# A 2-D transform pair rebuilt on a half spectrum with half-sample shift, in an adaLN block with its backward pass

## The chip, the cores and the metric

The program runs on one core of one Trainium2 chip. The metric is the device time of one execution in microseconds (us), as the median of several runs. Besides those runs there is one profiled execution; its rows are what this document reads. PE is TensorE (matmul), PEld its weight loads, DVE is VectorE, ACT ScalarE, POOL GpSimd, SP the engine that issues the DMAs. L12 is line 12 of the kernel.

## The reference

One block of a conditioned network and its whole gradient, S = 2048 positions, D = 512 features, F = 1792 hidden units, bf16:

```python
mod = silu(c) @ w_mod                # six rows of 512: sa, ca, ga, sb, cb, gb
h   = layernorm(x) * (1 + ca) + sa
y   = irfft2(rfft2(h) * (w_r + 1j*w_i))      # 2-D FFT over (2048, 512)
x1  = x + ga * y
h2  = layernorm(x1) * (1 + cb) + sb
out = x1 + gb * (relu(h2 @ w1 + b1)**2 @ w2 + b2)
```

It returns out and the gradients of x, w_r, w_i, w1, b1, w2, b2, c and w_mod for a given grad_out. The backward pass of the filter is the same kind of work as the forward one: a 2-D transform of the gradient of y, a product with the conjugate of the filter, and an inverse transform.

## The kernel before

Rows: position s = 16p + t, so x is 16 tiles ("rows", t) of 128 partitions by 512 features. The 2048-point transform over s is split in 128 x 16, and every step of it is a matmul against a table of cosines and sines.

*Constants.* `trig3_from_index` (L26) makes a cosine, a sine and a negative sine from a table of products of indices: scale, round to the nearest integer and subtract (VectorE), then ScalarE's Sin. `build_constants_pre` (L44) makes TA (128-point table, 5 x 128 columns), `build_constants_cd_lc` (L88) makes Cd (512-point table: cos, sin, -sin for 257 frequencies) and LC (the twiddles and the 16-point step in one, masked to blocks of 8), `build_constants_cf` (L133) makes Cf (inverse 512-point table). Their iotas run on GpSimd.

*Modulation* (L425 to L458): w_mod (3 MB) is loaded, six rows of 512 computed and broadcast over the partitions into `modb`.

*LayerNorm 1* (L479 to L492): per row a tensor_reduce on VectorE and a Square with a running sum on ScalarE, then a handful of ops for 16 rows at once with a square root on ScalarE. `h1_row` (L494) normalises one row on ScalarE, stores it to `n1_dram` and applies 1 + ca and sa with two tensor_tensor ops on VectorE.

*Forward transform.* Stage 1, `spec_stage_a` (L180): 16 rows x 4 feature chunks, each a matmul against 256 columns (cos and -sin of TA), each evicted from PSUM, VectorE and ScalarE in turn, into UT. Stages 2 and 3, `spec_stages_bc` (L196): for each of 16 frequency groups 16 matmuls of 257 columns (the 512-point step, real and imaginary apart), two evictions, 4 matmuls of 257 columns against LC, two evictions, and six VectorE ops of 257 columns for the complex product with the filter (`load_wf`, L255, scales the filter by a row `ef` first). In the backward pass the same function also makes the filter's gradients with six more.

*Inverse transform.* `spec_stage_a2` (L271): 16 groups x 3 frequency chunks, two matmuls of 256 columns each. `spec_stages_b2c2` (L289): for each of 16 rows 12 matmuls of 512 columns into psDr and psDi, an eviction of each (ScalarE, VectorE), two matmuls of 512 columns into psY, and the row's consumer. In the forward pass that is `y_cons` (L517): copy y, store it, x1 = x + ga*y, LayerNorm 2 of the row with a Square, a reduce and seven small ops, scale and shift, four transposes into h2T. In the backward pass it is `gh1_cons` (around L855 to L878): the gradient through LayerNorm 1, six VectorE ops of 512 columns and two column sums on TensorE.

*The rest*: MLP 1 (L560 to L584), MLP 2 with the loss side of the gradient (L588 to L650), the MLP's backward pass (L655 on; it begins with a 2 MB load of the normalised rows into n2b, L658, from which VectorE rebuilds h2b, L662, and with the matmuls psg, L681), the gradient of w1 (L780 to L805, its matmuls psw at L799), then the backward transforms (L812 to L880) and the gradients of w_mod by chunks (`emit_gmod_chunk`, L338). The tables live until MLP 2 has ended, are stored to DRAM after MLP 1 (`cs_dram`, L586) and reloaded before the backward transforms (L813).

*Order.* A planner lists each engine's instructions by its own estimate of when they are ready; an instruction whose data and memory are free may stand far ahead of its place in the text, DMAs above all. At run time every engine works through its list in order. Tiles that lie in the same memory at different times wait for one another; "left" and "right" are two ends of the on-chip memory from which pools are taken. All DMAs go through SP's queue.

## Time and profile before

| | |
|---|---|
| median of 3 runs | 847.06 us (845.75 to 848.27) |
| span of the profiled execution | 846.4 us, 10536 instructions; no time besides it is given for that execution |
| PE busy | 671.8 us (79%), 3600 instructions |
| DVE busy | 541.6 us (64%), 1569 |
| ACT busy | 328.4 us (39%), 695 |
| POOL busy | 5.0 us (1%), 17 |
| DMA | 87.71 MB, mean 104 GB/s |

The stages follow one another with little overlap: tables, modulation and LayerNorm sums (0 to 52 us), forward stage 1 (52 to 80), stages 2 and 3 (80 to 122), inverse first stage (122 to 143.5), inverse row loop (143.5 to 210), MLP 1 and 2 (210 to 332), a gap (332 to 350), MLP backward (350 to 645), then the same transform stages backward (645 to 676, 676 to 718, 718 to 743, 743 to 812) and the last chunks (812 to 846.4). The page's shares are of the whole span, so the stages are read one by one: a view of busy time by stretch gives the limit of each, the chain of waits what ended last, the timeline the pace of single instructions. Matmuls are pipelined; where a mean duration is above the pace, the pace is taken from starts that follow one another.

### The profile page before, as it was taken

The numbers are of one execution on the slowest core, as the hardware profiler recorded it, in microseconds if no ns is written. First come the engines' busy times: TensorE is split into PE (matmuls) and PEld (weight loads), VectorE is DVE, ScalarE is ACT, GpSimd is POOL, SyncE is SP. The second block draws the span as 40 slices with busy tenths as digits, with TensorE's granted clock in tenths as the row PEclk, the third lists the DMA queues.
The fourth block names the chain that finished last, engine by engine and source line by source line (L and its number), as shares of the span: only waits on it lengthen the run. The fifth ranks groups of instructions, "written<-read, shape, count | busy, mean of one in ns | idle before, by whom it ended". The sixth has DMA issues, their size and how long they took to land. (4 is left out here: it accounts for less than half of the span.)

```text
span 846.4 us, 10536 instructions
## 1 busy us (share of the span) xinstructions
PE 671.8 (79%) x3600; PEld 313.8 (37%) x3644; DVE 541.6 (64%) x1569; ACT 328.4 (39%) x695; POOL 5.0 (1%) x17
## 2 busy tenths in 40 slices
PE   3137988996999997599999789948997599699940
PEld 0013763332444433254444323305553277233300
DVE  7986875997444455845454369973123469879881
ACT  5985434786676311133333101124132335332210
POOL 1000000000000000000000000000000000000000
PEclk9555998997999999699999979957999599899955
DMA  6433003443634234422221543220154540200010
GB/s 256 180 130 111 34 1 113 135 136 122 239 148 174 87 94 160 145 69 88 69 88 44 67 145 112 88 74 12 39 192 182 168 189 2 100 13 32 31 50 25
DMA packets 56073, 87.71 MB, mean 104 GB/s; under 512 B 9810, under 2 KB 48596, under 8 KB 53972
## 3 DMA queue, kind: packets, MB, share of 16 engines
q1 hardware_dynamic: 56020, 87.05, 30.2%
q8 instruction: 28, 0.46, 0.2%
q14 instruction: 25, 0.20, 0.1%
HBM read 50.27 MB, written 36.76 MB: 103 GB/s over the span
## 5 line engine op out<-in xcount | busy, mean ns | idle before, releaser
L684 DVE SCALAR_TENSOR_TENSOR ghT<-rT_pf,twof,psg 128x512 bf16<-128x512 bf16 x56 | 40.7, 744 | 51.4 <-PE psg L681 51.2
L681 PE MATMUL psg<-gBT,w2T 128*128 128x512 bf16 x218 | 60.1, 389 | 2.3 <-ACT gwm L362 1.8
L740 PE MATMUL psh<-w1T,ghT 128*128 128x512 bf16 x218 | 55.5, 391 | 1.0 <-issue 0.5
L621 PE MATMUL psO<-w,hactT 128*128 128x512 bf16 x217 | 52.7, 379 | 1.1 <-ACT rT L580 0.8
L577 PE MATMUL psH<-h2T,w 128*128 128x512 bf16 x219 | 51.7, 386 | 2.1 <-ACT rT L580 1.0
L799 PE MATMUL psw<-ghn,h2b 128*128 128x448 bf16 x256 | 51.4, 354 | 0.0
L700 PE MATMUL psw<-gB,hnat 128*128 128x512 bf16 x216 | 50.2, 380 | 1.0 <-DVE hnat L697 0.5
L186 PE MATMUL psA<-TA,h1row 128*128 128x256 bf16 x64 | 18.8, 402 | 36.5 <-DVE h1row L501 33.8
L580 ACT ACTIVATE rT<-psH,b1col 128x512 bf16<-128x512 f32 x56 | 38.4, 687 | 15.8 <-PE psH L577 14.4
L581 DVE TENSOR_TENSOR hactT<-rT 128x512 bf16<-128x512 bf16 x56 | 23.8, 426 | 32.1 <-ACT rT L580 32.1
L702 ACT CAST gw<-psw 128x512 bf16<-128x512 f32 x14 | 8.2, 586 | 73.8 <-PE psw L700 63.2
L304 PE MATMUL psDi<-Cf,U2T 128*128 128x512 bf16 (+1 forms) x94 | 35.5, 378 | 0.1
L303 PE MATMUL psDr<-Cf,U2T 128*128 128x512 bf16 (+1 forms) x92 | 35.0, 381 | 0.5 <-ACT U2T L286 0.4
L740 PEld LDWEIGHTS <-ghT 128*128 128x128 bf16 x224 | 19.9, 99 | 40.4 <-issue 22.6
L743 ACT CAST gh<-psh 128x512 bf16<-128x512 f32 x16 | 9.4, 586 | 65.0 <-PE psh L740 65.0
L695 ACT COPY rnat<-pstr 128x512 bf16<-128x512 bf16 x56 | 29.9, 588 | 12.1 <-PE pstr L694 10.1
L303 PE MATMUL psDr<-Cf_reload,U2T 128*128 128x512 bf16 (+1 forms) x93 | 33.8, 381 | 0.9 <-ACT U2T L286 0.4
L304 PE MATMUL psDi<-Cf_reload,U2T 128*128 128x512 bf16 (+1 forms) x95 | 34.1, 379 | 0.1
L191 ACT CAST UT<-psA 128x256 bf16<-128x256 f32 x64 | 23.0, 371 | 27.7 <-PE psA L186 26.9
L577 PEld LDWEIGHTS <-w 128*128 128x128 bf16 x224 | 22.0, 98 | 31.2 <-issue 8.9
L799 PEld LDWEIGHTS <-h2b 128*128 128x128 bf16 x256 | 24.6, 98 | 20.8 <-issue 0.2
L303 PEld LDWEIGHTS <-U2T 128*128 128x128 bf16 (+1 forms) x192 | 17.9, 95 | 38.3 <-issue 24.5
(289 smaller groups left out, 1442.0 us busy)
## 6 DMA issues: line engine op xcount, KB each, us to landing
rT_dram<-rT SPq DMA_DIRECT2D x14, 512.0 KB, 2.6
rT_pf<-rT_dram SPq DMA_DIRECT2D x14, 512.0 KB, 3.4
w<-in_B_w_dram SPq DMA_DIRECT2D x2, 1792.0 KB, 7.2
wm<-in_w_mod_dram SPq DMA_DIRECT2D x1, 3072.0 KB, 10.2
wmc_pf<-in_w_mod_dram SPq DMA_DIRECT2D x6, 512.0 KB, 14.4
...
```

The costliest lines, as they stand in the source:

```text
L303: nc.tensor.matmul(psDr, lhsT=lhsT, rhs=Cf[:ksz, (0 if ri == 0 else 2), fs, :], start=(n == 0), stop=(n == 5))
L304: nc.tensor.matmul(psDi, lhsT=lhsT, rhs=Cf[:ksz, (1 if ri == 0 else 0), fs, :], start=(n == 0), stop=(n == 5))
L577: nc.tensor.matmul(psH, lhsT=w1[:, dc, fc * P:(fc + 1) * P], rhs=h2T[:, dc, sc * 4 * P:(sc + 1) * 4 * P], start=(dc == 0), stop=(dc == 3))
L580: nc.scalar.activation(rT[:, sc * 4 * P:(sc + 1) * 4 * P], psH, AF.Relu, bias=b1col[:, fc:fc + 1])
L581: nc.vector.tensor_tensor(hactT[fc][:, sc * 4 * P:(sc + 1) * 4 * P], rT[:, sc * 4 * P:(sc + 1) * 4 * P], rT[:, sc * 4 * P:(sc + 1) * 4 * P ...
L621: nc.tensor.matmul(psO, lhsT=hactT[fc][:, t * P:(t + 1) * P], rhs=w2[:, fc, :], start=(fc == 0), stop=(fc == NFC - 1))
L681: nc.tensor.matmul(psg, lhsT=w2T[:, dc, fc * P:(fc + 1) * P], rhs=gBT[:, dc, sc * 4 * P:(sc + 1) * 4 * P], start=(dc == 0), stop=(dc == 3))
L684: nc.vector.scalar_tensor_tensor(out=ghT[fc][:, sc * 4 * P:(sc + 1) * 4 * P], in0=rT[:, sc * 4 * P:(sc + 1) * 4 * P], scalar=K["twof"], in ...
L695: nc.scalar.copy(out=rnat[:, 4 * tg:4 * tg + 4, :], in_=pst.rearrange("p (j f) -> p j f", j=4))
L700: nc.tensor.matmul(psw2, lhsT=hnat[:, t, :], rhs=gB[:, t, :], start=(t == 0), stop=(t == NT - 1))
L740: nc.tensor.matmul(psh, lhsT=ghT[fc][:, t * P:(t + 1) * P], rhs=w1T[:, fc, :], start=(fc == 0), stop=(fc == NFC - 1))
L799: nc.tensor.matmul(psw, lhsT=h2[:, t, dc * P:(dc + 1) * P], rhs=ghn[:, t, cc * 448:(cc + 1) * 448], start=(t == 0), stop=(t == NT - 1))
```

## The change

Both transforms are computed on a half spectrum with a half-sample shift. The 512-point step uses angles 2 pi f (d + 1/2) / 512; cosines of even index and sines are each 256 columns, so the real input gives 512 real columns and not 2 x 257 complex ones, and the first step over s (TA) is one real table of 128 columns (`build_ta`), of which TAT is the transpose for the last step. Frequency groups go in pairs (g, 16 - g); LF and LG hold the twiddles with the combination of a pair, 6 and 3 tables of 16 x 128 and 16 x 256 columns. All tables are made from integer indices (multiply, add, bitwise and) and one Sin with a bias.

- Constants: `build_basic`, `build_ta`, `build_cd`, `build_cf`, `build_lf`, `build_lg` take the place of the three builders. GpSimd makes iotas, masks and small vectors.
- x is loaded first, in four pieces; w_mod after it, in four.
- LayerNorm 1 and 2: `bn_stats` and `bn_aggr` on VectorE, `rstd` (an add and a power -0.5) on GpSimd, one tensor_scalar (subtract, multiply) on VectorE.
- 1 + ca, sa and ga are multiplied into the tables CdF (forward) and CdB (backward); sa enters through one extra matmul of one row. 1 + cb and sb are applied in the eviction of the transposed rows. The modulation is computed after stage 1.
- Stage 1 `spec_f1`, stages 2 and 3 `spec_f23` with `cmul`, inverse `spec_g1` and `spec_g23` take the place of the four `spec_stage...` functions.
- LF, LG, CdB and Cf (7.3 MB) are stored right after they are built and reloaded in the backward pass (before: 3.7 MB). The tables' memory is released before the hidden activations are allocated.
- Backward: g_x1 is loaded in four pieces and used directly as the input of stage 1; before, its rows were loaded a second time and multiplied by ga. n1 is loaded in the pool of the last stage. The spectrum Xs is stored to DRAM by group.

The MLP and its backward pass are not edited, but for the release of the tables. The core of the diff:

```diff
-        for t in range(NT):
-            nc.vector.tensor_reduce(ssum[:, t:t + 1], x_sb[:, t, :], axis=AX.X, op=ALU.add)
-            nc.scalar.activation(n1junk, x_sb[:, t, :], AF.Square, accum_out=ssq[:, t:t + 1])
+        def n1_row(t):
+            nc.vector.bn_stats(st, x_sb[:, t, :])
+            nc.vector.bn_aggr(mv, st)
+            rstd(nc, inv1[:, t:t + 1], mv[:, 1:2], K)
+            nc.vector.tensor_scalar(n1row, x_sb[:, t, :], mv[:, 0:1], inv1[:, t:t + 1], op0=ALU.subtract, op1=ALU.mult)
+            nc.sync.dma_start(n1_dram[:, t, :], n1row)
+            return n1row
+def rstd(nc, dst, var, K):
+    nc.gpsimd.tensor_scalar(dst, var, 1e-5, None, op0=ALU.add)
+    nc.gpsimd.tensor_tensor(dst, dst, K["nhalf"], op=ALU.pow)
...
+def build_lf(tc, K, cpool, g):
...
+    for nm, off in (("c", 1536.0), ("s", 1024.0)):
+        v = g.tile([P, 16, P], I32, name=f"lf_v{nm}")
+        nc.vector.tensor_scalar(v, kr, tf, off, op0=ALU.mult, op1=ALU.add)
+        nc.vector.tensor_single_scalar(v, v, 2047, op=ALU.bitwise_and)
+        w = g.tile([P, 16, 16, 8], BF16, name=f"lf_{nm}")
+        nc.scalar.activation(w.rearrange("p g a b -> p g (a b)"), v, AF.Sin, scale=TWO_PI / 2048, bias=K["npi"])
+        tr.append(w)
...
+    for y, (w, m) in enumerate(((c, 0), (s, 1), (s, 2), (c, 2), (c, 1), (s, 3))):
+        nc.vector.tensor_tensor(L5[:, y], w, mk[:, m, :, None, :].broadcast_to([P, 16, 16, 8]), op=ALU.mult)
...
+def spec_f1(tc, K, row, UT):
...
+            ps = psA_pool.tile([P, 4, P], FP32, name="psA")
+            for c in range(4):
+                nc.tensor.matmul(ps[:, c, :], lhsT=hrow[:, c * P:(c + 1) * P], rhs=K["TA"], start=True, stop=True)
+            if t % 2 == 1:
+                nc.scalar.copy(out=dst, in_=src)
+            else:
+                nc.vector.tensor_copy(out=dst, in_=src)
+def spec_f23(tc, K, UT, Cd, dc, dest, elementwise):
...
+        def f3(gi):
+            ae = AEs[gi % 3]
+            for g in pair_of(gi):
+                ps = psC_pool.tile([P, 2, 512], FP32, name="psC")
+                for o, ys in ((0, (0, 1, 2, 3)), (1, (1, 4, 3, 5))):
+                    for n, y in enumerate(ys):
+                        ri, e = n // 2, n % 2
+                        nc.tensor.matmul(ps[:, o, 0:DF], lhsT=LF[:, y, g, :], rhs=ae[:, ri, 256 * e:256 * e + DF],
+                                         start=(n == 0), stop=(n == 3))
+                nc.scalar.copy(out=dest(g), in_=ps[:, :, 0:DF])
+            elementwise(gi)
+        for gi in range(8):
+            for ri in range(2):
+                for c in range(4):
+                    nc.tensor.matmul(ps[:, ri, :], lhsT=UT[:, c, ri * 8 + gi, :, :], rhs=Cd[:, c, :],
+                                     start=(c == 0), stop=(c == 3 and not extra))
...
+            nc.scalar.copy(out=dst, in_=ps.rearrange("p r (e f) -> p r e f", e=2))
+            if gi > 0:
+                f3(gi - 1)
+        f3(7)
+def cmul(nc, pool, A, B, gi, outr, outi, conj_a, nm):
+    sl = pair_slice(gi)
+    nc.vector.tensor_tensor(p1[:, :, :, 0:DF], A[:, sl, :, 0:DF], B[:, sl, :, 0:DF], op=ALU.mult)
+    nc.vector.tensor_tensor(p2[:, :, :, 0:DF], A[:, sl, :, 0:DF], B[:, sl, ::-1, 0:DF], op=ALU.mult)
+    nc.vector.tensor_tensor(outr[:, sl], p1[:, :, 0, 0:DF], p1[:, :, 1, 0:DF], op=(ALU.add if conj_a else ALU.subtract))
+    nc.vector.tensor_tensor(outi[:, sl], p2[:, :, 0, 0:DF], p2[:, :, 1, 0:DF], op=(ALU.subtract if conj_a else ALU.add))
+def spec_g1(tc, K, Z, CS):
...
+        for gi in range(8):
+            for e in range(2):
+                for ch in range(2):
+                    for g in pair_of(gi):
+                        for ri in range(2):
+                            nc.tensor.matmul(ps[:, ch, :], lhsT=Z[:, g, ri, f0:f0 + P],
+                                             rhs=LG[:, e + ri, g].rearrange("p r t b -> p (r t b)"),
+                                             start=(n == 0), stop=(n == 3))
+def spec_g23(tc, K, CS, consumer):
...
+        def g3(t, Tsb):
+            psY = psY_pool.tile([P, D], FP32, name="psY")
+            nc.tensor.matmul(psY, lhsT=K["TAT"], rhs=Tsb, start=True, stop=True)
+            consumer(t, psY)
+        for t in range(NT):
+            for c in range(4):
+                nc.tensor.matmul(ps, lhsT=CS[:, t, c].rearrange("p r a b -> p (r a b)"), rhs=K["Cf"][:, c, :],
+                                 start=(c == 0), stop=(c == 3))
+            nc.scalar.copy(out=Tsb, in_=ps)
+            if prev is not None:
+                g3(*prev)
...
+            rstd(nc, inv2[:, t:t + 1], mv[:, 1:2], K)
+            nc.vector.tensor_scalar(n2rows[:, t % 4, :], x1row, mv[:, 0:1], inv2[:, t:t + 1], op0=ALU.subtract, op1=ALU.mult)
+            if t % 4 == 3:
...
+                    if dc % 2 == 0:
+                        nc.vector.tensor_scalar(dst, src, cbcol[:, dc:dc + 1], sbcol[:, dc:dc + 1], op0=ALU.mult, op1=ALU.add)
+                    else:
+                        nc.scalar.activation(dst, src, AF.Identity, scale=cbcol[:, dc:dc + 1], bias=sbcol[:, dc:dc + 1])
...
-                def u_row(t):
-                    nc.sync.dma_start(gr, gx1_dram[:, t, :])
-                    nc.vector.tensor_tensor(ur, gr, modb[:, 2, :], op=ALU.mult)
+            spec_f1(tc, K, lambda t: g_x1[:, t, :], UT)
```

## Rows read from the trace of the kernel before

**Rows 1.** Busy time by stretch: span, PE, PEld, DVE, ACT, POOL (instructions), clock, DMA, GB/s
```profile
0.00:52.00 52.00, 9.07 (x30) 2.53 (x30) 45.37 (x121) 41.24 (x92) 4.98 (x17) 0.74 0.53 208
52.00:80.00 28.00, 18.77 (x64) 7.11 (x65) 24.13 (x64) 21.83 (x48) 0.00 (x0) 0.50 0.22 76
80.00:122.00 42.00, 40.27 (x321) 31.92 (x321) 29.20 (x108) 15.65 (x47) 0.00 (x0) 0.96 0.14 51
...
143.50:210.00 66.50, 58.08 (x282) 22.65 (x289) 55.67 (x201) 47.08 (x105) 0.00 (x0) 0.95 0.39 123
...
645.00:676.00 31.00, 15.98 (x64) 6.58 (x63) 17.25 (x45) 11.64 (x32) 0.00 (x0) 0.63 0.59 215
...
743.00:812.00 69.00, 64.44 (x248) 20.41 (x254) 59.45 (x164) 18.37 (x32) 0.00 (x0) 0.96 0.08 27
812.00:846.40 34.40, 6.54 (x12) 1.17 (x11) 14.38 (x42) 3.52 (x6) 0.00 (x0) 0.50 0.12 38
```

**Rows 2.** Chain that ended last, in order of time: start, us, what ran
```profile
588.54 20.63 PE psw L799 x109
...
649.51 13.50 DMA gx_row<-gx_dram
...
704.35 0.21 DVE wt L242
...
804.10 0.75 DVE v L874
804.85 0.67 DVE gn L864 x2
805.52 0.34 DVE gx L877
805.86 0.67 DVE qn L867 x2
...
806.77 0.32 DVE v L872
807.10 0.61 DVE Dsb L308
```

**Rows 3.** Timeline of PE in backward stage 2: start, duration, instruction
```profile
684.02 0.27 PE L209 MATMUL psBr<-Cd_reload,UT 128*128 128x257 bf16 x1
684.13 0.27 PE L210 MATMUL psBi<-Cd_reload,UT 128*128 128x257 bf16 x1
```

**Rows 4.** DMA issues: what, queue, KB each, median us from issue to landing
```profile
x_sb<-in_A_x_dram SPq DMA_DIRECT2D x1, 2048.0 KB, 15.0
```

**Rows 5.** Groups by line: count, busy us, mean ns of one, idle before it
```profile
L480 DVE TENSOR_REDUCE l_sum<-x_sb 128x1 f32<-128x512 bf16 x16 | 10.4, 679 | 0.0
...
L29 DVE TENSOR_SCALAR trig_t<-ang 128x512 f32<-128x512 f32 x4 | 1.7, 419 | 0.0
...
L697 DVE TENSOR_TENSOR hnat<-rnat 128x2048 bf16<-128x2048 bf16 x14 | 17.1, 1220 | 0.1
...
L307 ACT CAST Dsb<-psDr 128x512 bf16<-128x512 f32 x32 | 18.7, 583 | 30.6 <-PE psDr L303 28.3 <-DVE c L869 2.1
```

**Rows 6.** Timeline of the set-up, POOL and DVE
```profile
2.12 0.67 POOL L121 IOTA ang_i<- 128x512 int32 x1
2.24 0.63 DVE L79 TENSOR_SCALAR m<-m,pidf 128x128 f32<-128x128 f32 x1
...
3.55 0.21 DVE L31 TENSOR_SCALAR trig_r<-trig_t 128x128 f32<-128x128 f32 x1
...
5.50 0.74 POOL L121 IOTA ang_i<- 128x512 int32 x1 [1.83 <-DVE ang L123]
```

**Rows 7.** Timeline between MLP 2 and the MLP's backward pass
```profile
331.49 0.32 SPq L658 DMA_DIRECT2D n2b<-n_dram  x1
...
341.04 0.76 DVE L662 TENSOR_TENSOR h2b<-n2b,modb 128x512 bf16<-128x512 bf16 x2 [2.09 <-DMA n2b<-n_dram]
...
348.88 2.72 PE L681 MATMUL psg<-gBT,w2T 128*128 128x512 bf16 x6 [1.83 <-ACT gwm L362]
```

More of the change, by code (lines that the diff above doesn't have):

```diff
@@ L15 @@
 I32 = mybir.dt.int32
-MAGIC = 12582912.0
+PSUM = bass.MemoryType.PSUM
 S = 2048
@@ new lines, in build_ta @@
+    nc.gpsimd.memset(off[:, 8:16, :], 0)
+    nc.gpsimd.memset(off[:, 8, 0:1], 96)
+    v = g.tile([P, P], I32, name="ta_v")
+    nc.vector.scalar_tensor_tensor(out=v, in0=kh.rearrange("p a b -> p (a b)"), scalar=K["pidf"],
+                                   in1=off.rearrange("p a b -> p (a b)"), op0=ALU.mult, op1=ALU.add)
+    nc.vector.tensor_single_scalar(v, v, 127, op=ALU.bitwise_and)
+    TA = cpool.tile([P, P], BF16, name="TA")
+    nc.scalar.activation(TA, v, AF.Sin, scale=TWO_PI / 128, bias=K["npi"])
@@ L271, in spec_stage_a2 @@
[L271 to L283 removed]
+    sm = g.tile([P, 16, 8], FP32, name="lf_sm")
@@ new lines @@
+    x_early = tc.alloc_tile_pool(name="xearly", bufs=1)
+    x_sb = x_early.tile([P, NT, D], BF16, name="x_sb")
+    for i in range(4):
+        nc.sync.dma_start(x_sb[:, 4 * i:4 * i + 4, :], x_view[:, 4 * i:4 * i + 4, :])
+    modp = tc.alloc_tile_pool(name="modw", bufs=1)
+    ccol = modp.tile([P, 4], BF16, name="ccol")
+    crow = modp.tile([1, D], BF16, name="crow")
+    with nc.allow_non_contiguous_dma(reason="tiny"):
+        nc.sync.dma_start(ccol, c.rearrange("b (dc p) -> p (b dc)", p=P))
+        nc.sync.dma_start(crow, c)
```

770 lines of the change are left out of this document (381 added, 389 removed).

## The prediction

> **What bounds the kernel now.** I read the busy shares first, then the busy time by stage, then the chain of waits, and last the order of instructions in three short stretches. The whole-span shares (TensorE 79%) say little, because the middle of the program, from 210 to 645 us, is one long run of dense matmuls that the change does not edit. The edited part is the rest: 210 us in front and 201 us behind. There the stages have different limits [rows 1]. From 0 to 52 TensorE works 9 us, and VectorE 45.4: VectorE is the bound, building tables and LayerNorm sums. From 52 to 80 (first transform stage) VectorE is busy 24 of 28 and TensorE has its low clock, 0.50 of 2.4 GHz. From 80 to 122 TensorE is the bound, 40.3 of 42 at clock 0.96. From 143.5 to 210 and from 743 to 812 (inverse transform with its per-row work) both are near full: the row work on VectorE is 55.7 of 66.5 and 59.5 of 69, TensorE 58 and 64. In the backward first stage, 645 to 676, neither is: the chain has one 13.5 us wait for a row of gx_dram [rows 2].
>
> The steady paces I use. Backward row loop on VectorE, from the chain [rows 2]: v2 0.75, gn 0.67, gx 0.34, qn 0.67, two small ops 0.24 (806.53 to 806.77), v1 0.32, PSUM cast Dsb 0.61; with q as gx 0.34 that is 3.9 us, and 16 rows are 63 of the 69 us. So a 512-wide bf16 tensor_tensor costs 0.34, a 512-wide PSUM cast 0.61, a two-scalar tensor_scalar 0.32. A 257-wide tensor_tensor costs 0.21, so by the slope a 1028-wide one 0.61 [rows 2]. TensorE at the high clock: 448 columns 20.63/109 = 0.19 [rows 2], so 512 columns 0.216; 257 columns each 0.11, 256 the same [rows 3].
>
> **The change part by part.** *TensorE.* Per transform pair before: 64 matmuls of 256 columns, 320 of 257, 96 of 256, 224 of 512. After: 64 of 128, then 64 of 512 and 128 of 257 (13.8 + 14.1 = 28 us), 128 of 256 (14.1), 80 of 512 (17.3). At the high clock 101 us become 63, twice. This is not the saving: each stage gets a new limit.
>
> *Set-up and first stage, forward (S1).* x is now first in the queue, in four pieces, and no longer behind the 3 MB of w_mod; its load took 15.0 us from issue to landing [rows 4]; now its first quarter is there at about 4.5 (estimate: 0.5 MB at the 208 GB/s of that stretch [rows 1] is 2.5 us, and a start of 2). LayerNorm per row on VectorE: bn_stats, bn_aggr, one tensor_scalar, half an eviction of 512. bn_stats is in no row: between 0.32 (one tensor_scalar pass) and 1.22 (two passes at the pace of tensor_reduce, 679 ns alone [rows 5], some 0.61 in a row of ops); I take 0.6, since it reads each element once like the reduce. bn_aggr between 0.08 and 0.3: 0.15. Sum 0.6 + 0.15 + 0.32 + 0.31 = 1.38, 16 rows 22 us. Then the tables that the forward stage 2 needs. Cd: four integer scalar_tensor_tensor of 512 (0.61 each), one 2048-wide AND, three 2048-wide scalings: 8 us. Modulation columns and rows: 3.5. LF: four 2048-wide integer passes and six 2048-wide products: 4.6 + 6 x 1.14 + 0.6 = 12. A 2048-wide integer pass is in no row: 1.14 by the 512-wide f32 tensor_scalar (419 ns: 0.15 and 0.27 for the columns) and 2.2 at the pace of the reduce; a product is 1.14 to 1.22 by hnat and 2.6 by four casts [rows 5]. I take the low ends, as same-width operands have them in these rows. Sum 22 + 8 + 3.5 + 12 + 2 = 47.5. VectorE was busy 87% of 0 to 52; 47.5/0.87 + 4.5 = 59. ScalarE, with some six 2048-wide sines, has under 25 us of work and is covered.
>
> *GpSimd.* The trace shows what GpSimd does to VectorE: while a 128x512 iota ran from 2.12 to 2.79, a 128x128 tensor_scalar took 0.63; right after, one of the same shape took 0.21 [rows 6]. The change gives GpSimd the masks, iotas and 32 pairs of tiny ops for the reciprocal root: at the 0.67 us of a 512-wide iota about 18 us of set-up work, where before it had 5 [rows 1]. I charge a quarter, 4 us, to VectorE; the bounds are 0 and 18. So LF is ready at 63. The Trainium skill (SBUF — State Buffer, Who interferes with whom) says that GpSimd and VectorE share one port pair as an exclusive lock, taken by VectorE's two-port modes and, for reads, by every two-input op; the rows above agree. By it every one of GpSimd's 18 us would count where VectorE runs tensor_scalar or copy, and the sum would end at 752 and not 738.
>
> *Stage 2, forward (S2).* Stage-2 matmuls of the first three groups can run before LF is there; behind it stand 16 products of 8 matmuls (14.1) and five groups of 1.73: 23, with the first microseconds at the low clock and the last eviction 26, so 89. VectorE has LG (six products, 7, and 3 of small ops) and Cf (5, as Cd without the integer ops of 0.61) left at 63, so until 78, then 8 groups of complex products, each two of 1028 and two of 514 columns, 2 x 0.61 + 2 x 0.34 = 1.9: 15. That is 93, with some idle 95. The products need W: its 2.1 MB and the 3.1 MB store of LF are 25 us at 208 GB/s, so 88 if both start at 63; I cost it nothing, since W's memory is free before LF is done and its loads can go ahead of the store; else it is 10 (rival B). The last group alone waits for it; stage 3 (14.1 on TensorE) ends at max(89 + 15, 95 + 3) = 104. Before: 143.5.
>
> *Row loop, forward (S3).* VectorE per row before: four bf16 ops of 0.34, reduce 0.6, Dsb 0.61, six small ops of 0.12, half an eviction 0.17: 3.46. After: ytmp and x1 0.68, bn_stats 0.6, bn_aggr 0.15, normalise 0.32, and two evictions of 512 per four rows 0.3 = 2.05. Before, 3.46 of work took 66.5/16 = 4.16 (83%) [rows 1]; at that share 2.47, 16 rows 39.5, with the chain of the first and of the last row 47. The normalise op now waits for GpSimd twice; behind it on VectorE stand the next rows' statistics and the evictions, and TensorE's transposes wait for those. I charge nothing, since three buffers let the next row's ops stand ahead; uncovered it is 16 x 0.6 = 10 (0.3 an op, between nothing and the 0.74 of GpSimd's longest op [rows 6]). ScalarE 1.45 per row (512-wide casts 0.58 [rows 5]) lies beside. MLP 1 starts at 104 + 47 = 151, not 210: **-59**.
>
> *Middle (S4).* No line of it is edited, but the tables leave the right side of memory before the hidden activations take it. Before, n2b lay under the activations, so its 2 MB load was issued only at 331.49, VectorE sat in order behind it until 341.04, the output row copies were late, and the first backward matmul came at 348.88 [rows 7]. Now n2b lies elsewhere and can load long before. What is late next is the chain of four copies through one buffer, each behind its store, an estimate of 2 us after the first: 343. **-5.6** (bounds 0 and -8).
>
> *Backward (S5).* g_x1 is now loaded first and used directly; the modulation product and the per-row loads behind 7 MB of other loads go. Loads start as before, an estimate of 3 us ahead of the row wait at 649.51 [rows 2], at 646.5; 2 MB in quarters, PE at the low clock 0.43 per row: the first stage ends at 657.5, not 676. The larger tables (7.3 MB, before 3.7) reload over memory that the transposes free, half of it once the w1 gradient is under way [rows 2], so I cost them nothing; if all wait until 645 they cost 10. Stage 2: VectorE 8 x 3.8 = 30 from 666, so 696.5; TensorE 691.5. The stage-3 buffer lies over Xs and waits for 696.5; it ends at 709 (before 743). Row loop: 3.9 - 0.61 = 3.3 at the old share of 90%, 16 rows 58.5: 767.5, not 812. **-44.5**. The tail of 34.4 us [rows 1] stays.
>
> Sum on the profiled span: 846.4 - 59 - 5.6 - 44.5 = 737.3. The page gives no time around the span; the runs' median is 847.06, 0.7 more, so **738**.
>
> **Rivals.** (A) Set-up stays VectorE-bound harder: integer passes and table products at one element a cycle (+6 and +9) or all of GpSimd's work in its way (+14): 753. For it: the 0.63 us op; against it: f32 and int32 casts of 512 run at 0.41. (B) Data arrives late behind: the W and Xs tiles now have 258-wide rows, so their loads go in 514-byte runs, and W may be 10 late in front; behind, stage 3 may wait for the two gradient stores, 2.1 MB, 10 us at 208 GB/s. One and a half of the three: 753. Against: their memory is free early. (C) Better: bn_stats at 0.4 and row loops at 90% share: 718. (D) The clock. TensorE has less work than VectorE in the new loops; 52 to 80 shows 0.50 with TensorE busy 18.8 of 28 [rows 1]. If stages 2 and 3 of both passes stay at 1.2 GHz, 28 + 14 more each: 738 + 84 = 822. Against: 80 to 122, equally dense, has 0.96. The skill (TensorE: Matmul & The Clock Gate, Loop structure matters more than you think) also puts this on the loop nest; here the nest keeps groups of 8 to 16 matmuls together. (E) Slower: the reciprocal root on GpSimd. Each of 32 rows waits for an add and a power; GpSimd's longest op took 0.74 [rows 6], none is a power. If VectorE, in order, waits for every pair, it decides at (847 - 738)/32 = 3.4 us a pair: at 4 us 866. Nothing in the rows is that long, and four or three buffers let other rows pass.
>
> **How the numbers follow.** Forecast 0.52, A 0.20, B 0.10, C 0.13, D 0.02, E 0.03. The range takes in A, B and C: the low end is C with n2b at its best (716), the high end A with half of B and most of the uncovered hop in two loops (775). D and E lie outside. A change under 0.3% (2.5 us) can't be told from none here. Only E, or several of A, B and D at once, ends above 847: slower 0.04, same 0.01, faster 0.95.
>
> **What would show it.** S1: the first stage-2 product (with LF) near 63; VectorE the busiest engine before it. S2: stage 3 done near 104. S3: MLP 1's first matmul near 151, VectorE per row about 2.6. S4: the first matmul of the backward MLP 5 to 6 us sooner after the last output row. S5: first stage 11 us from its loads, stage 3 done 63 us after them, row loop 58. I am wrong if GpSimd's busy time in the row loop fills it, if VectorE waits for GpSimd over 1 us a row, if the clock in stages 2 and 3 is under 0.8, or if the gain sits in TensorE's columns alone.

## The result and the profile after

The changed kernel takes 770.3 us (769.85 to 772.14, four runs) where the kernel before takes 846.4 on the same chip: a ratio of 0.9115, 95% interval 0.9087 to 0.9143. The profiled span is 770.4 us (before 846.4), so 76 us are gone where 109 were forecast on the span. Direction and place were right; 33 us of the forecast gain did not arrive, and the study is about them. The runs below were made beside other measurements of the kernel before (844 to 849 us), so they are compared by their ratios to it, and a difference of medians alone under some 4 us says little.

Busy time by stretch, changed kernel; columns as in [rows 1]:

```profile
0.00:56.30 56.30, 20.62 (x121) 10.01 (x122) 47.38 (x119) 23.37 (x29) 30.46 (x86) 0.99 0.36 131
56.30:74.40 18.10, 6.58 (x18) 1.94 (x17) 14.80 (x39) 7.09 (x5) 4.55 (x17) 0.59 0.87 318
74.40:102.20 27.80, 27.12 (x177) 18.16 (x178) 13.34 (x28) 15.70 (x23) 0.00 (x0) 0.91 0.95 214
102.20:117.00 14.80, 14.15 (x128) 12.52 (x128) 7.47 (x13) 4.68 (x8) 0.00 (x0) 1.00 0.59 161
117.00:167.10 50.10, 26.26 (x145) 11.66 (x145) 32.95 (x89) 23.03 (x40) 13.44 (x32) 0.80 0.54 166
167.10:227.50 60.40, 55.35 (x232) 23.15 (x232) 33.33 (x87) 38.32 (x56) 0.00 (x0) 0.91 0.52 189
...
537.90:605.40 67.50, 60.94 (x422) 34.98 (x420) 13.20 (x28) 16.71 (x30) 0.00 (x0) 0.98 0.35 135
605.40:628.20 22.80, 6.39 (x65) 5.30 (x64) 5.63 (x9) 3.97 (x7) 0.17 (x3) 0.63 1.02 298
628.20:665.50 37.30, 31.16 (x220) 21.11 (x219) 30.75 (x65) 17.57 (x26) 0.00 (x0) 0.96 0.08 19
665.50:686.50 21.00, 13.52 (x104) 11.22 (x104) 5.44 (x8) 4.68 (x8) 0.00 (x0) 0.74 0.52 201
686.50:737.30 50.80, 34.28 (x111) 9.24 (x111) 47.75 (x148) 17.65 (x32) 0.00 (x0) 0.87 0.10 35
737.30:770.40 33.10, 6.07 (x11) 1.09 (x10) 14.45 (x43) 3.51 (x6) 0.00 (x0) 0.50 0.13 42
```

Read it against [rows 1]. The stretches in which one engine is nearly always busy are those that came out as forecast or shorter: set-up (VectorE 47.38 us, forecast 47.5), backward stage 2 (VectorE 30.75, forecast 30), forward stage 3 (TensorE busy 14.15 of 14.80, forecast 14.1) and the backward row loop, which was shorter. Four other stretches, in which no engine is near full, lost time: 56 to 74, the forward loop (VectorE 33 of 50), 605 to 628 (TensorE 6.4, VectorE 5.6 of 22.8) and the front of 665 to 686. In two of these the DMA share is 0.87 and 1.02: there data or memory may be late and not work, which the timelines below can tell.

Two stretches of the timeline of the changed kernel, ahead of stage 2 and in MLP 1 (start, duration, engine, instruction, idle time before it and what ended that):

```profile
71.54 1.66 DVE L150 TENSOR_SCALAR Cf<-cf_sn,cf_ef 128x512 bf16<-128x512 f32 x4
73.31 1.93 ACT L333 CAST AE<-psB 128x1024 bf16<-128x1024 f32 x2 [5.98 <-DVE Cf L150]
73.60 1.25 SPq L395 DMA_DIRECT2D W<-in_A_w_i_dram  x1
74.38 3.62 PE L317 MATMUL psC<-AE,LF 128*128 128x257 bf16 x16 [11.52 <-ACT AE L333]
...
86.31 0.70 DVE L403 TENSOR_TENSOR fp<-Xs,W 128x1028 bf16<-128x1028 bf16 x1 [13.11 <-ACT Xs L319]
...
187.96 0.76 DVE L765 TENSOR_TENSOR h2b<-n2b,modb 128x512 bf16<-128x512 bf16 x2 [2.85 <-DMA n2b<-n_dram]
189.37 1.26 ACT L686 ACTIVATE rT<-psH,b1col 128x512 bf16<-128x512 f32 x2 [4.71 <-DMA rT_dram<-rT]
190.10 36.71 PE L683 MATMUL psH<-h2T,w 128*128 128x512 bf16 x152 [4.37 <-ACT rT L686]
```

LF was ready at 56.3, and stage 2 began at 74.38. The eviction AE waited 5.98 us for Cf, a table that stage 2 does not read: AE's buffers lie over the scratch memory in which Cf is built. This is the last wait of the 18.1 us and not the whole of them; the first experiment shows what stands before it. In MLP 1 the wait belongs to a 2 MB load (n2b) which stands in SP's queue between the stores of rT, so ScalarE finds no free rT buffer.

Chain of waits of the changed kernel, from the w1 gradient to stage 3 (start, us, what):

```profile
593.45 8.23 DMA out_dram<-gw
...
606.35 10.25 DMA out_dram<-gw
617.04 4.53 DMA g_x1b<-gx_dram
...
665.63 5.97 DMA out_dram<-gWi
671.70 0.59 ACT CSb L360
672.33 13.53 PE psG L351 x104
```

Stores of 112 KB take 8 to 10 us beside the table reloads. VectorE can't evict the next block. The load of g_x1 is issued only when the last of these stores has landed, at 616.7: 11 us after TensorE ran out of work at 605.3. The first product of stage 1 follows at 621.8.

Groups of the forward row loop, 117 to 165, VectorE (count, busy us, mean ns, idle before):

```profile
L644 DVE BATCH_NORM_STATS2 l_st<-x1row 128x6 f32<-128x512 bf16 x16 | 10.9, 688 | 0.1
L651 DVE TENSOR_SCALAR n2rows<-x1row,l_mv,inv 128x512 bf16<-128x512 bf16 x16 | 6.6, 413 | 12.4 <-POOL inv L389 12.4
```

12.4 us in 16 waits for GpSimd's reciprocal root, 0.77 us a row.

Where the 33 us are, by the prediction's own steps (measured minus forecast, in us): S1 and S2 +12.3 (stage 3 done at 116.3, not 104: S1 6.7 early, S2 19.0 late); S3 +3.8 (50.1 from 117.0 to MLP 1, in place of 47, with the rest at the joint); S4 +8.0 (from MLP 1's first matmul to the backward MLP's first: 141.2, not 133.2); MLP backward -2.3; w1 gradient +4.4 (67.4, before 63.0); S5: first stage +9.2 (22.9 us after the last w1 matmul, not 13.7), stage 2 -1.6, stage 3 +7.5 (20.1 after the last complex product, not 12.5), row loop -6.8; tail -1.3. Sum +33.2, and 737.3 + 33.2 is 770.5. It is a net: 51.9 us are late, and 18.7 came out shorter than forecast.

### The profile page after: what moved, and what is told of

It is laid out like the page before. It is cut to its first block, busy times and chain, and to the rows that moved or that the text cites. A ratio compares the mean times of both kernels' runs of the same rounds, so it can differ in the third digit from the quotient of the medians.

```text
span 770.4 us, 9001 instructions
## 1 busy us (share of the span) xinstructions
PE 576.6 (75%) x3190; PEld 278.1 (36%) x3190; DVE 445.3 (58%) x1126; ACT 251.4 (33%) x404; POOL 48.6 (6%) x138
## 5 line engine op out<-in xcount | busy, mean ns | idle before, releaser
L683 PE MATMUL psH<-h2T,w 128*128 128x512 bf16 x224 | 55.1, 402 | 5.2 <-ACT rT L686 4.4
L843 PE MATMUL psh<-w1T,ghT 128*128 128x512 bf16 x224 | 56.3, 392 | 0.4 <-DVE ghT L787 0.4
L803 PEld LDWEIGHTS <-hnat 128*128 128x128 bf16 x224 | 20.8, 98 | 29.4 <-DVE hnat L800 6.2
L784 PEld LDWEIGHTS <-w2T 128*128 128x128 bf16 x224 | 21.1, 99 | 23.2 <-issue 6.9
L909 DVE CAST gw<-psw 128x448 bf16<-128x448 f32 x8 | 5.0, 624 | 42.3 <-PE psw L902 25.3
L725 PEld LDWEIGHTS <-hactT 128*128 128x128 bf16 x224 | 20.2, 98 | 24.6 <-issue 4.2
L730 DVE TENSOR_TENSOR bo<-psO,b2b 128x512 bf16<-128x512 f32 x16 | 11.1, 691 | 27.6 <-PE psO L725 27.6
L891 PE MATMUL pstg<-ident,ghT 128*128 128x128 bf16 x224 | 21.0, 242 | 7.7 <-DVE ghn L893 4.0
```

Source lines behind the costliest of these rows:

```text
L683: nc.tensor.matmul(psH, lhsT=w1[:, dc, fc * P:(fc + 1) * P], rhs=h2T[:, dc, sc * 4 * P:(sc + 1) * 4 * P], start=(dc == 0), stop=(dc == 3))
L725: nc.tensor.matmul(psO, lhsT=hactT[fc][:, t * P:(t + 1) * P], rhs=w2[:, fc, :], start=(fc == 0), stop=(fc == NFC - 1))
L784: nc.tensor.matmul(psg, lhsT=w2T[:, dc, fc * P:(fc + 1) * P], rhs=gBT[:, dc, sc * 4 * P:(sc + 1) * 4 * P], start=(dc == 0), stop=(dc == 3))
L803: nc.tensor.matmul(psw2, lhsT=hnat[:, t, :], rhs=gB[:, t, :], start=(t == 0), stop=(t == NT - 1))
L843: nc.tensor.matmul(psh, lhsT=ghT[fc][:, t * P:(t + 1) * P], rhs=w1T[:, fc, :], start=(fc == 0), stop=(fc == NFC - 1))
L891: nc.tensor.transpose(pst[:, jj * P:(jj + 1) * P], ghT[fc][:, t * P:(t + 1) * P], K["ident"])
```

## The experiments

Theory: the engines do what was forecast, and the missing 33 us are waits for memory that is still in use and for transfers queued behind others; each goes when its cause goes. A wait "stands behind" another when it ends later, so that taking the first away shows only part of its price. Rivals, by run: that another limit stands right behind the wait; that the DMA engines' bytes, not the order, are short; that TensorE's saved columns are the gain; that LayerNorm is.

**AE in memory of its own.** The buffers are allocated ahead of the scratch.

```diff
+    aef = tc.alloc_tile_pool(name="aef", bufs=1)
     lgp = tc.alloc_tile_pool(name="lgp", bufs=1)
-        AEs = [aep.tile([P, 2, 514], BF16, ...) for i in range(3)]
+        AEs = [(aep_in or aep).tile([P, 2, 514], BF16, ...) for i in range(3)]
```

> The three AE buffers of the forward stage 2 get memory of their own, ahead of the scratch of the LG and Cf tables; nothing else is changed. Theory (memory, not LF or TensorE, delays the forward stage 2): in the changed kernel LF is ready at 56.3 us but the first product with it starts at 74.4, just behind the last Cf op at 73.2, whose scratch the AE buffers lie over. With memory of their own that product starts at 58 to 62, TensorE is through stage 2 by about 88, the complex products still wait for the second half of W (86.3 now), end near 101.5, and stage 3, which needs them pair by pair, ends near 104 and not 116: 770.3 becomes 757 to 760. Rival 1 (W alone is the bound, stage 3 can't overlap it): stage 3 ends at 115 to 117, 769 to 771. Rival 2 (stage 2 is held by TensorE or by the Cf and LG ops themselves): the first product stays near 74, 770.

Measured: 773.2 us, ratio to before 0.9103 (0.9084 to 0.9122): no gain, where 757 to 760 was expected; the first rival came true. Stage 2 did begin sooner, at 68.3 (expected 58 to 62), and was done at 95.7, but the first complex product now waited for W. Timeline of this kernel:

```profile
61.33 2.11 ACT L273 ACTIVATE lg_c<-lg_vc,npi 128x2176 bf16<-128x2176 int32 x1 [8.16 <-DVE lg_vc L271]
63.34 2.09 ACT L273 ACTIVATE lg_s<-lg_vs,npi 128x2176 bf16<-128x2176 int32 x1
65.34 1.99 ACT L147 ACTIVATE cf_sn<-cf_v,npi 128x2048 f32<-128x2048 int32 x1
67.23 1.90 ACT L333 CAST AE<-psB 128x1024 bf16<-128x1024 f32 x2
68.28 3.62 PE L317 MATMUL psC<-AE,LF 128*128 128x257 bf16 x16 [6.22 <-ACT AE L333]
...
88.46 0.70 DVE L403 TENSOR_TENSOR fp<-Xs,W 128x1028 bf16<-128x1028 bf16 x1 [15.26 <-DMA W<-in_A_w_i_dram]
```

W's second half is issued at 73.6 as before and lands at 88.5 (86.3 in the changed kernel), so stage 3 still ran from 96.6 to 115.5. The AE wait was real, and a second stood right behind it. The edit also shows a third, which no run takes away: AE has memory of its own here, TensorE had made its input by 62.1, and yet ScalarE evicts it at 67.23, because three sines of the tables LG and Cf stand ahead of it in ScalarE's list. TensorE is idle for 6.22 us meanwhile. Had the eviction been put ahead of these sines, stage 2 could have begun some 6 us sooner (an estimate from these rows, not run).

**AE in its own memory, and W's load ahead of the table stores.** The edit above, and the four stores of tables moved behind the issue of W.

```diff
-    for key in ("LF", "LG", "CdB", "Cf"):
-        nc.sync.dma_start(cs_dram[key], K[key])
...
+        for key in ("LF", "LG", "CdB", "Cf"):
+            nc.sync.dma_start(cs_dram[key], K[key])
         spec_f23(tc, K, UT, CdF, ...
```

> As e1 (AE buffers in memory of their own), and the four table stores stand behind the loads of W. In e1 the first product with LF came at 68.3 and not 74.4, TensorE was through stage 2 at 95.7, but the complex products waited for the second half of W until 88.5 (its load was issued at 73.6, behind the stores of LG and Cf, and took 14.8 us), so stage 3 still ended at 115.5. Theory (two waits, one behind the other; both have to go): W lands at 68 to 72, the complex products follow the evictions, TensorE runs stages 2 and 3 without a gap and ends at 109 to 112; MLP 1 starts 4 to 7 us sooner; ratio to before 0.903 to 0.908, 763 to 768. Rival (the table stores are late instead and hold back the row loop's small loads): no gain, 770 or more.

Measured: 768.5 us, 0.9052 (0.9026 to 0.9077), at the upper end of what was expected (763 to 768). First product with LF at 69.5, stage 3 from 97.8 to 111.7, MLP 1 at 162.8, 4.3 us sooner; by the ratios 5.3 us are gained. The two waits lay one behind the other: AE's edit alone showed nothing. W's move alone was not run; in the changed kernel TensorE is busy 27.12 of 27.80 us from 74.4 and 14.15 of 14.80 behind it, so there W had hardly anything to give by itself.

**Gradient stores by group.** gWr and gWi are stored in sixteen pieces each as their groups come out of the complex product.

```diff
                     cmul(nc, ew, Xs, G, gi, gWr, gWi, True, "b")
+                    for g in pair_of(gi):
+                        nc.sync.dma_start(out2_view[:, g], gWr[:, g, :])
+                        nc.sync.dma_start(out3_view[:, g], gWi[:, g, :])
-                nc.sync.dma_start(out2_view, gWr)
-                nc.sync.dma_start(out3_view, gWi)
```

> The two filter gradients are stored group by group while stage 2 of the backward pass runs, not in two stores of 1 MB at its end. Theory (rival B of the prediction: the stage-3 buffer lies over the gradients and waits for their stores; the chain shows 6.0 us of the gWi store ahead of it): stage 3 ends 5 to 7 us sooner after the last complex product, 764 to 766. Rival (stage 3 would then wait as long for the Xs and W memory or for n1): 769 to 771. Rival (32 small stores in the queue delay the loads of that stretch): 772 or more.

Measured: 772.1 us, 0.9100 (0.9072 to 0.9127): no gain, where 764 to 766 was expected. Timeline, VectorE:

```profile
668.66 1.29 DVE L358 CAST CSb<-psG 128x512 bf16<-128x512 f32 x2 [5.06 <-DMA out_dram<-gWr]
```

The wait fell from 6.2 to 5.06 us only: the last small store, issued at 664.64, still lands at 668.6. Smaller stores helped by 1 us only; not to wait for a store could help more.

**Stage 3 without a wait for the stores.** CS becomes a view of UT's memory, whose data is dead by then; the gradients move to a pool that outlives stage 3, and their stores stand behind the load of n1.

```diff
-            CS = su3.tile([P, NT, 4, 2, 8, 8], BF16, name="CSb")
+            CS = UT.rearrange(...)
-            gWr = sx.tile([P, NT, DF], BF16, name="gWr")
+        gWr = sa.tile([P, NT, DF], BF16, name="gWr")
...
+            nc.sync.dma_start(out2_view, gWr)
+            nc.sync.dma_start(out3_view, gWi)
             spec_g1(tc, K, Z, CS)
```

> In the backward pass the stage-3 result lies over the stage-1 result UT (read for the last time at 653) and not over the filter gradients; the gradient stores go behind the n1 load, which goes in four pieces. Theory (the wait is for memory, and smaller stores did not shorten it by more than 1 us because the last one still takes 4): stage 3 runs beside the complex products pair by pair and ends at 668 to 674, not 685.6; n1, whose memory is free at 665.5, is late next; 755 to 762. Rival (VectorE takes the evictions only behind its complex products, 14 us of stage 3 stay uncovered): stage 3 ends at 677 to 681, 763 to 767. Rival (n1 decides): 768 or more.

Measured: 766.1 us, 0.9046 (0.9013 to 0.9078). Stage 3 ends 12.1 us after the last complex product (20.1 before this edit; forecast 12.5). Timeline:

```profile
668.37 1.88 DVE L358 CAST UTb<-psG 128x512 bf16<-128x512 f32 x3
669.11 11.43 PE L351 MATMUL psG<-LG_reload,Zb 128*128 128x256 bf16 x88 [3.50 <-DVE UTb L358]
```

This is the first rival's time and not the theory's 755 to 762. What is left, 3.5 us, is what that rival named: VectorE takes its share of the evictions only behind its last complex products.

**The reciprocal root once per four rows.** In the second LayerNorm GpSimd's add and power work on 128x4 in place of 128x1.

```diff
-            nc.vector.tensor_scalar(n2rows[:, t % 4, :], x1row, mv[:, 0:1], inv2[:, t:t + 1], ...)
+            if t % 4 == 3:
+                nc.gpsimd.tensor_scalar(iv, mv[:, :, 1], 1e-5, None, op0=ALU.add)
+                nc.gpsimd.tensor_tensor(iv, iv, K["nhalf"].broadcast_to([P, 4]), op=ALU.pow)
+                for j in range(4):
+                    nc.vector.tensor_scalar(n2rows[:, j, :], n2g["x"][j], mv[:, j, 0:1], iv[:, j:j + 1], ...)
```

> In the forward row loop the reciprocal root is made once for four rows (GpSimd gets 4 pairs of ops and not 16), and the four rows are normalised together. Theory (VectorE waits for the round trip to GpSimd once per row, 12.4 us of idle time in 16 waits of 0.77): 4 waits are left, some 3 us; the loop of 49.4 us falls to 40 to 44, less up to 3 for the later last group: 762 to 767. Rival (the wait only fills time in which VectorE would wait for ScalarE's or TensorE's results): the idle time moves to other releasers, 769 to 772.

Measured: 770.1 us, 0.9056 (0.9026 to 0.9086). Groups, VectorE, forward loop:

```profile
L657 DVE TENSOR_SCALAR n2rows<-x1row,l_mv,inv 128x512 bf16<-128x512 bf16 x16 | 5.5, 408 | 4.8 <-POOL inv L655 3.4 <-DMA x1row_o<-x_dram 1.5
```

The wait for GpSimd fell from 12.4 to 3.4 us, the loop from 50.1 to 46.5. Part of the rest moved: the wait for ScalarE's yrow grew from 3.8 to 5.7, and 2.4 us are new before rows of x. The loop was expected at 40 to 44, the time at 762 to 767; the medians show no gain, the ratios one of 5 us.

**n2b in four pieces, four rT buffers.**

```diff
-    nc.sync.dma_start(n2, n2_dram)
+    for i in range(4):
+        nc.sync.dma_start(n2[:, 4 * i:4 * i + 4], n2_dram[:, 4 * i:4 * i + 4])
-    tc.tile_pool(name="rtp", bufs=2)
+    tc.tile_pool(name="rtp", bufs=4)
```

> The 2 MB load of n2b goes in four pieces, and the MLP 1 output has four store buffers and not two. Theory (the n2b load that came free early now collides with the MLP 1 stores: TensorE has a gap of 4.4 us at 186 to 190 while ScalarE waits 4.7 us for an rT store and VectorE 2.9 us for n2b): the gap goes, MLP 1 takes 53 to 55 us and not 59.3, 764 to 767. Rival (the gap is lost DMA bandwidth and only moves by the same amount): 769 to 772.

Measured: 766.1 us, 0.9021 (0.8998 to 0.9045). Busy time of MLP 1:

```profile
167.40:220.30 52.90, 52.61 (x232) 22.47 (x232) 32.67 (x87) 38.47 (x56) 0.00 (x0) 0.97 0.59 215
```

TensorE is busy 52.61 of 52.90; in the changed kernel it was 55.35 of 60.40 with the same 232 matmuls. The collision was the whole loss of MLP 1 itself. The pieces and the buffers were changed together, so this run does not say which of the two was needed.

**Stores and the g_x1 load on ScalarE's queue.**

```diff
-                    nc.sync.dma_start(out4_view[:, dc, f0:f0 + 448], gw1)
+                    nc.scalar.dma_start(out4_view[:, dc, f0:f0 + 448], gw1)
-            nc.sync.dma_start(g_x1[:, 4 * i:4 * i + 4], ...)
+            nc.scalar.dma_start(g_x1[:, 4 * i:4 * i + 4], ...)
```

> The stores of the w1 gradient (gw) and the four g_x1 loads are issued from ScalarE's queue and not from SP's; nothing else is changed. Theory (order in one queue: the reloads of LF, LG, Cf and Xs, 8.2 MB issued from 581 on, stand ahead of four gw stores that take 8 to 10 us each where they took 1.7; VectorE then waits for its buffer, TensorE's last w1 matmuls end 4 us late, and g_x1, whose memory waits for the last gw store, is issued at 616.7, 11 us after the last matmul): with a queue of their own the stores take 2 to 4 us, the w1 gradient ends 3 to 4 us sooner and the first stage 8 to 12 us sooner, 758 to 763. Rival (the 16 engines are full, 0.87 busy, and share whatever queue asks): the stores still take 7 us or more, 767 to 772.

Measured: 772.8 us, 0.9122 (0.9107 to 0.9138): no gain. Timeline:

```profile
583.03 0.34 ACTq L911 DMA_DIRECT2D out_dram<-gw  x1
...
594.83 0.62 DVE L909 CAST gw<-psw 128x448 bf16<-128x448 f32 x1 [11.83 <-DMA out_dram<-gw]
```

The store issued at 583.0 frees VectorE's buffer at 594.8, 11.8 us later, and the evictions wait 31.7 us in all for such stores (31.6 in the changed kernel). The reloads became slower too (LG 17.7 us from issue to landing, 13.8 in the changed kernel). So the two queues share what carries the bytes. The Trainium skill (DMA: Bandwidth & Descriptors, Queues, rings and completion order) says so: SP and ACT each own one ring on each of the same 16 DMA engines, which take turns between rings packet by packet; these numbers agree with the sharing, while the taking of turns is not seen in them. The load of g_x1 was issued 5.5 us sooner (611.2) and stage 3 ended 2.3 us sooner, yet the time shows no gain: the stretch behind the last row of the tail was longer here (30.0 us, 27.4 in the changed kernel), and that part differs between runs.

**LG and Cf reloaded behind g_x1.** CdB and LF are reloaded as before, the two others after the g_x1 loads; a one-column copy of g_x1's last row into each of them holds their reloads back until g_x1 is there.

```diff
-        nc.sync.dma_start(tl, cs_dram[key])
+        if key in ("CdB", "LF"):
+            nc.sync.dma_start(tl, cs_dram[key])
...
+        nc.vector.tensor_copy(K["LG"][:, 0, 0, 0, 0, 0:1], g_x1[:, NT - 1, 0:1])
+        nc.vector.tensor_copy(K["Cf"][:, 0, 0:1], g_x1[:, NT - 1, 0:1])
+        for key in ("LG", "Cf"):
+            nc.sync.dma_start(K[key], cs_dram[key])
```

> The reloads of LG and Cf (3.6 MB) are held back until the last quarter of g_x1 has landed, by a one-column copy from g_x1 into each; LF, CdB and Xs stay where they are. Theory (bytes ahead in the queue): the gw stores behind LG and Cf (8.2 and 10.3 us now) take under 4 us, that behind LF stays near 8; the first stage ends 5 to 8 us sooner, 762 to 766; LG lands near 640 and is needed near 657, so it costs nothing. Rival (LF and Xs alone keep the queue full): 768 to 771. Rival (LG becomes late for stage 3): 772 or more.

Measured: 778.7 us, 0.9195 (0.9177 to 0.9214): slower, by 8.4 us by the medians and 6.8 by the ratios. The evictions' waits for stores fell from 31.6 to 18.5 us and stage 1 began 2.6 us sooner (619.2), but then W stood behind LG. Timeline, VectorE:

```profile
639.69 0.70 DVE L403 TENSOR_TENSOR bp<-Wb,G 128x1028 bf16<-128x1028 bf16 x1 [13.64 <-DMA Wb<-in_A_w_i_dram]
```

In the changed kernel that product started at 635.2. To move a reload moves the wait.

**The LayerNorm edit alone.** The kernel before, with bn_stats, bn_aggr and GpSimd's root in both LayerNorms and nothing else of the change.

```diff
+            nc.vector.bn_stats(st, x1row)
+            nc.vector.bn_aggr(mv, st)
+            rstd(nc, inv2[:, tp:tp + 1], mv[:, 1:2], K)
+            nc.vector.tensor_scalar(n2row, x1row, mv[:, 0:1], inv2[:, tp:tp + 1], op0=ALU.subtract, op1=ALU.mult)
```

> The kernel before with one part of the change: both LayerNorms by bn_stats, bn_aggr, the reciprocal root on GpSimd and one tensor_scalar on VectorE, transforms and tables as before. Theory (the gain is in the transforms and tables; in the set-up VectorE, the bound, gets 0.6 us a row more work than tensor_reduce and ScalarE less; in the row loop TensorE is near full): between 838 and 856 against 847. Rival (LayerNorm is a large part of the gain of 76 us): 800 to 830.

Measured: 857.7 us against 847.7, 1.0116 (1.0091 to 1.0141): slower by 10, just outside what was expected. Stage 1 ends at 84.7 (before 79.3), MLP 1 begins at 220.2 (before 210.1), and the loop waits 9.5 us for GpSimd. This part of the change is a loss by itself.

**The psT sums twice.** Every psT sum of the two row loops is made by eight matmuls in place of four, each operand twice, some 27.6 us more of TensorE over both passes. The second matmul with c equal to 0 starts the sum anew, so the values stay what they were.

```diff
-            for c in range(4):
+            for c in (0, 1, 2, 3, 0, 1, 2, 3):
                 nc.tensor.matmul(ps, lhsT=CS[:, t, c]..., rhs=K["Cf"][:, c, :], start=(c == 0), stop=(c == 3))
```

> In the row loops of both passes each psT sum of four 512-column matmuls is made twice (the first result is overwritten), 128 more matmuls of 512 columns, 27.6 us of TensorE at 0.216. Theory (the new row loops are bound by VectorE: 3.25 us a row in the backward one, 2.3 and a GpSimd round trip in the forward one, TensorE 1.7 and 2.0): 0 to 5 us longer, 770 to 776. Rival (TensorE's columns were the limit and are what the change saved): 20 to 28 us longer, 790 to 798.

Measured: 783.6 us, 0.9228 (0.9207 to 0.9248): 13 us over the changed kernel by the medians, 0.0113 of the time before, some 9.6, by the ratios to the kernel before. The forward loop grew by 5.6, the backward one by 2.0; the rest lies in neither. Busy time of the forward loop in this kernel:

```profile
116.00:171.70 55.70, 37.74 (x209) 17.39 (x209) 34.91 (x89) 23.17 (x40) 13.21 (x32) 0.95 0.48 149
```

So most of 27.6 us of TensorE is hidden, yet more than the theory's 0 to 5 shows; the rival's 20 to 28 is refuted. It is no clean price of a column: with the added matmuls the granted clock of this loop rose from 0.80 to 0.95, so the other matmuls can have run faster than before and given part of the cost back.

**All that paid, together.** AE and W, the root by four rows, n2b and rT, CS over UT; and all backward stage 3 evictions on ScalarE, for the 3.5 us seen above.

```diff
-                if e == 0:
+                if e == 0 and not act:
                     nc.vector.tensor_copy(out=dst, in_=src)
...
-            spec_g1(tc, K, Z, CS)
+            spec_g1(tc, K, Z, CS, act=True)
```

> The changed kernel with e2, e5, e8 and e4c together, and in the backward pass all stage-3 evictions on ScalarE, so that they don't stand behind VectorE's complex products. Theory (the waits found lie one after the other in time and add up): 6 for e2, 4 for e5, 5 for e8, 6 for e4c and 5 to 8 for ScalarE's evictions, less up to 4 where the next wait shows: 742 to 750. Rival (they share a cover, DMA or VectorE time, and give half): 755 to 762.

Measured: 742.0 us (740.6 to 745.8), 0.8755 (0.8723 to 0.8787). Expected were 742 to 750. Backward stage 3 runs from 638.0 to 652.1 without a gap. Chain of waits, what is left at the end of the w1 gradient:

```profile
587.41 10.06 DMA out_dram<-gw
597.61 4.73 DMA g_x1b<-gx_dram
```

**Eight gw buffers.** With eight in place of two, VectorE's evictions were to find a free buffer at once. The buffers go to the right side of memory, so that g_x1 does not lie over them either; the two prefetches of w_mod columns, whose memory that is, move behind backward stage 2.

```diff
-tc.tile_pool(name="bwF2", bufs=2) as bfq
+tc.tile_pool(name="bwF2", bufs=8, side="right") as bfq
-        wmc0 = prefetch_wmc(tc, wm_view, 0, sa)
-        wmc1 = prefetch_wmc(tc, wm_view, 1, sa)
...
+            wmc0 = prefetch_wmc(tc, wm_view, 0, su3)
+            wmc1 = prefetch_wmc(tc, wm_view, 1, su3)
             spec_g1(tc, K, Z, CS, act=True)
```

> best1, with eight and not two buffers for the w1 gradient's stores, on the other side of memory, so that neither VectorE's evictions nor the memory of g_x1 wait for those stores (in best1 they take 8 to 10 us each behind 8 MB of reloads, and g_x1 is issued 11 us after the last w1 matmul); the loads of w_mod's chunks for the tail go behind stage 2. Theory (the stores' memory is what stalls, the bytes alone cost less): the w1 gradient ends 3 to 5 us sooner, g_x1 lands 7 to 12 us sooner, W is late next (it lands near 608 in best1's time, needed at 601); 732 to 737, ratio 0.862 to 0.869. Rival (the bytes are the bound: the engines are 0.9 busy from 562 to 613 whatever waits): 739 to 743, ratio 0.872 or more.

Measured: 726.5 us (725.4 to 730.1), 0.8614 (0.8584 to 0.8645), below the 732 to 737 expected. Timeline around the g_x1 load, and busy time by stretch:

```profile
557.79 20.78 PE L911 MATMUL psw<-ghn,h2b 128*128 128x448 bf16 x109
580.16 2.15 SPq L932 DMA_DIRECT2D g_x1b<-gx_dram  x4
585.85 5.71 PE L291 MATMUL psA<-TA,g_x1b 128*128 128x128 bf16 x52 [7.28 <-DMA g_x1b<-gx_dram]
605.22 0.70 DVE L403 TENSOR_TENSOR bp<-Wb,G 128x1028 bf16<-128x1028 bf16 x1 [12.09 <-ACT AE L333]
```

```profile
110.60:155.00 44.40, 25.96 (x143) 13.11 (x145) 32.14 (x90) 23.34 (x40) 5.34 (x8) 0.80 0.64 195
155.00:207.00 52.00, 51.49 (x227) 22.36 (x232) 32.83 (x87) 38.02 (x56) 0.00 (x0) 0.97 0.58 214
515.40:578.20 62.80, 59.89 (x422) 34.54 (x420) 13.20 (x28) 16.77 (x30) 0.00 (x0) 1.00 0.36 134
578.20:593.40 15.20, 7.10 (x66) 6.01 (x64) 6.10 (x9) 4.68 (x8) 0.17 (x3) 0.66 0.94 287
593.40:635.40 42.00, 41.79 (x315) 31.17 (x320) 30.18 (x64) 25.60 (x39) 0.00 (x0) 1.00 0.28 68
635.40:690.00 54.60, 38.22 (x112) 9.37 (x112) 48.08 (x149) 18.26 (x34) 0.00 (x0) 0.78 0.37 130
```

The w1 gradient is back at 62.8 us, as before the change. One eviction, on ScalarE, still waits 5.5 us for a store, but TensorE does not. g_x1's load is issued 2 us after the last matmul and not 11, with every table reload still made. The run changed three things at once: how many buffers there are, where they lie, and when the w_mod columns are loaded. It shows that the waits go with them, not which of the three it takes. From 593 to 635 TensorE is busy 41.79 of 42.00, where the changed kernel took 58.3 for the same two stages. On the spans (770.4 to 723.3) the 47 us are: front 12, MLP stretch 10, w1 gradient 5, backward stage 1 8, stages 2 and 3 16, and 4 lost again in the row loop, into which the w_mod prefetches now fall (one store of a row takes 8.0 us there, of which 3 are on the chain of waits). The 6 us in which AE stands behind the sines are still there: the first product with LF starts at 68.29, with TensorE idle for 5.45 us before it.

## Why the prediction was right, and where it was not

**Right: the work.** VectorE's busy time to LF (47.38; 47.5 forecast), backward stage 2 (30.75 on VectorE) and backward stage 3 once it had started (13.5 us of matmuls; 12.5 forecast to its end) came out as worked from [rows 1, 2, 5]. bn_stats is 0.67 to 0.69 us by its record, 0.58 from one to the next in a row of them (taken: 0.6), bn_aggr 0.16 (0.15), the 2048-wide integer passes and products 1.2 to 1.3 (1.14: the low end was the right one). LF was ready at 56.3, before the 63 forecast: the 4 us charged for GpSimd weren't needed, although it worked 30.5 us and not 18. The Trainium skill (SBUF — State Buffer, Who interferes with whom) lets GpSimd's time count wherever VectorE wants the shared port; one row may bear it out (one 512-wide normalisation took 0.87 us beside GpSimd's iotas and memsets, where most take 0.41), but the whole of set-up shows no such sum.

**Wrong, S2 (19.0 us from LF, of which LF's earlier end hides 6.7): "behind it stand 16 products".** "It" is LF: the step took the table and VectorE as the only gates of stage 2. AE's memory lay over the scratch of later tables (5.98 us of wait for Cf, which stage 2 does not read). Behind that, AE's eviction had its place in ScalarE's list after three sines of LG and Cf, 6 us that S1 had put at nothing ("has under 25 us of work and is covered"): an engine with time to spare still holds an eviction if its list has other work first. And the second half of W, of which the step said "I cost it nothing, since W's memory is free before LF is done and its loads can go ahead of the store", was issued at 73.6. W is rival B's first half; moving AE's memory and W gave 4.3 us at MLP 1. With the root by four rows as well the best kernel's MLP 1 begins at 155.0, near the 151 forecast.

**Wrong, S3 (3.8 us): the hop to GpSimd "I charge nothing".** 12.4 us of VectorE's wait, 0.77 a row, a little over the uncovered price that was given (10). Some of it is filled by other idle time: taking 9 us of it away gave 3.6. Rival E (866) fell: a pair takes 0.87 us, not 3.4.

**Half right, S4: -5.6.** From the last output row to the first backward matmul it is 12.2 us in place of 17.8, exactly -5.6. But the early n2b load, which gave this, stands in front of the rT stores, and MLP 1 grew from 53.0 to 59.3. The step followed the load to where it left, not to the queue that it joined. In four pieces and with four buffers it costs nothing.

**Wrong, S5: "reload over memory that the transposes free, half of it once the w1 gradient is under way [rows 2], so I cost them nothing; if all wait until 645 they cost 10".** They cost 13.6 (w1 gradient 4.4, first stage 9.2) by not waiting: 8 to 10 us of each small store, two buffers, VectorE and then g_x1's load behind them. In the best kernel, with six more buffers, other places for them and later w_mod loads, 12.3 of the 13.6 are gone. The other loss, 7.5, is stage 3 behind the gradient stores, rival B's second half, seen and given 10% of the chance. The row loop was better than forecast by 6.8. The step took 3.3 us of VectorE a row at 90% busy, 3.66 us a row; the rows follow one another at 3.25 us with VectorE never idle between them. That this offsets losses elsewhere is luck.

**The other rivals.** The clock (D) is 0.91 and 1.00 in forward stages 2 and 3, 0.96 and 0.74 in the backward ones; over backward stage 3 it fell under the 0.8 that the prediction gave as a sign. The low figures are of stretches that hold waits: 0.59 from 56 to 74, and 0.74 takes in 6 us of wait (0.85 from 672.3 to 686.5, while the matmuls ran). But from 56.3 to 62.9 TensorE was busy 6.57 of 6.60 us at 0.56, behind a wait of 3.3 us. That cost nothing that shows here, as the eviction of these results waited until 73.3 for other reasons. A's integer passes at one element a cycle did not come. So the work came out as forecast, and the waits did not: the sum held next to none, and the stretches with them came out 51.9 us late. That the total is only 33 off is luck, 18.7 us of other stretches being shorter than forecast. The time lies in the upper part of the stated range, whose high end was A with half of B and most of the uncovered hop: the hop and B's halves came, but in A's place stood waits that no rival had priced. With most of the waits removed the time is 726.5, below the 738 forecast, which the stretches that came out shorter make possible.

That the LayerNorm edit alone costs 10 us was not a step of the prediction, which credited it inside S3. The gain of the change must then come from its other parts, or from LayerNorm only together with them; no run tells the two apart.
